# Eight transposes moved up SyncE's queue in a fused attention and mixer kernel

## The chip, the cores and the metric

The kernel runs on one core of one Trainium2 chip. The metric is the device time of one execution in microseconds. Five engines with a queue each take part: TensorE (PE, matmuls), VectorE (DVE), ScalarE (ACT), GpSimd (POOL, here mostly the issuer of loads that cast from float32 to bfloat16) and SyncE (SP, here the issuer of all DMA transposes and of the stores). All DMAs share the core's 16 DMA engines; the page lists SyncE's as queue q1 and GpSimd's as queue q0.

## The reference, cut to what matters

Eight batches of 3008 tokens. First a gated attention without softmax, then an MLP mixer over tokens and channels:

```python
scores = scale * np.matmul(z, z.transpose(0, 2, 1))    # z: (8, 3008, 64)
attn = np.maximum(scores, 0.0) ** 2
x = u * np.matmul(attn, v)                             # u, v: (8, 3008, 256)
h = np.maximum(x.transpose(0, 2, 1) @ w_tok1, 0.0) @ w_tok2    # d_tok = 256
y = x + h.transpose(0, 2, 1)
out = y + np.maximum(y @ w_ch1, 0.0) @ w_ch2           # d_ch = 1536
```

## The kernel before, in words

The 3008 tokens of a batch are cut into `NQ = 6` query blocks of 512 (the last has 448), and the keys into `NG = 6` groups of the same size. A block of scores (one query block, one key group) is made in two pieces of 1024 columns: TensorE multiplies (`sc`, L457), ScalarE takes the relu into a buffer `at` (L495), VectorE squares it in place (L503). Six `at` buffers go round. TensorE then multiplies the block by v into the accumulators of the query block (L684). Scores are symmetric, so from the second batch on a block above the diagonal is computed once and its mirror image is made by a DMA transpose on SyncE (`flip`, L550, issue at L554), from `at` into a buffer `fl`. The `at` buffer is free when its own product and its transpose are done. In batch 0 every block is computed directly.

When a query block is complete, VectorE adds its halves and multiplies by u (`gate`, L818 and L838), which gives `xT`. SyncE transposes this x (`turn_x`, L870, issue at L875, into `x_pair`), and VectorE makes sums of it (`x_sums`, L912, into `d_pair`); both feed the token mixer, which starts when the last block of the batch is done (`tok1`, L1017).

Inputs reach the core by GpSimd and are turned by SyncE: `load_z` (L129) and `turn_z` (L141, and L145 for the last tile), `load_u` (L248) and `turn_u` (L258); `load_v` (L220) and the weights (L267 to L289) are only loaded. `after` (L124) has GpSimd copy one column of a tensor into `mark`, so that everything behind it in GpSimd's queue waits until that tensor is there.

The order on each engine is written by a planner when the program is built: it keeps a model of the engines' times and emits instructions in the order that the model gives. Loads and turns do not come out of the model; they are hung on steps of the attention by hand. `at_group(n, f)` runs f when the planner begins group n, where n counts blocks of scores times v: `base` is the batch's first, `q * NG` the query block's. The engines themselves take the instructions of their queue strictly in that order and wait on semaphores, so the hand-set step decides only the place in the queue. `turn_u` for query blocks 2 to 5 of batch 0 and `turn_next_z` (the two halves of z of batch 1) are such steps. So is this list of loads, which is spread over steps from `begin` on and stands behind one mark:

```python
    items = [lambda c=c: load_v(1, c) for c in vorder]
    items += [lambda c=c: ask_w_tok1(c) for c in range(NG)]
    items += [lambda c=c: ask_w_tok2(c) for c in range(NG)]
    items += [lambda part=part: ask_w_ch(part) for part in range(4)]
    items += [lambda m=m: load_u(m // NQ, m % NQ) for m in (NQ, NQ + 1)]
    begin = 2 * NG + 3
    at_group(begin, lambda: after(zTs[1][:, KT, :1]))
```

The later u loads of batch 1 (`ask_u`) wait each for a mark and for a `ur` buffer, of which there are two, each free when its turn has landed. The program's functions are long; the ones that the text speaks of are those named here.

Of the kernel before, what the change touches and what calls it, by code (L numbers as in the profile page):

```python
# [57 lines left out]
def kernel(  # L58
# [22 lines left out]
    NQ = (S + QW - 1) // QW  # L81
    NG = KT // GK
# [39 lines left out]
    def after(column):  # L122

        nc.gpsimd.tensor_copy(mark[:column.shape[0], :1], column)  # L124

    def load_z(b, c):
        n = full_tiles[c]
        k = c * GK + 1
        nc.gpsimd.dma_start(out=zs[:, k:k + n, :], in_=rows_of(z[b], c))  # L129
        if n < GK:  # L130
            for r in range(2):
                nc.gpsimd.dma_start(
                    out=zs[r * TAIL:(r + 1) * TAIL, k + n, :], in_=last_rows(z[b]))
        loading(LOAD / 4)

    def turn_z(zT, half):


        n = KT // 2
        for k in (half * n, half * n + 1):  # L140
            nc.sync.dma_start_transpose(  # L141
                out=zT[:, k:k + n:2, :],
                in_=zs[:, k:k + n, :].rearrange("p t d -> p (t d)"))
        if half:
            nc.sync.dma_start_transpose(  # L145
                out=zT[:, KT, :], in_=zs[:, KT:, :].rearrange("p t d -> p (t d)"))
# [97 lines left out]
    def load_u(b, q):  # L244
        tag, n = u_home(b, q, "ur")
        ur = sb.tile([P, QW // P, D], BF16, tag=tag, name="ur", bufs=n)
        n = full_tiles[q]
        nc.gpsimd.dma_start(out=ur[:, :n, :], in_=rows_of(u[b], q))  # L248
        if n < QW // P:
            nc.gpsimd.memset(ur[TAIL:, n, :], 0.0)  # L250
            nc.gpsimd.dma_start(out=ur[:TAIL, n, :], in_=last_rows(u[b]))
        urs[b, q] = ur
        loading(LOAD)

    def turn_u(b, q):
        ur = urs.pop((b, q))
        uT = new_uT(b, q)
        nc.sync.dma_start_transpose(  # L258
            out=uT.rearrange("p t h s -> p (t h) s"),
            in_=ur.rearrange("p t d -> p (t d)"))  # L260
        on_sp(1.25)
        if b == 0 and q > 1:
            release("fl", [1], free["sp"] + 4.0)
# [1227 lines left out]
    def new_zT(b):  # L1491
        zTs[b] = sb.tile([P, KT + 1, P], BF16, tag="zT", name="zT", bufs=2)
# [12 lines left out]
    def on_sp(us):  # L1505
        start = max(free["sp"], pe[0])
        free["sp"] = start + shared(start, us)

    def turn_next_z(b, half):
        turn_z(zTs[b + 1], half)  # L1510
        on_sp(2.8 + 1.2 * half)

        for c in range(NG // 2 * half, NG // 2 * (half + 1)):
            turned[b + 1, c] = Done(pe[0] + 10.0)
        if half:
            turned[b + 1, NG // 2 - 1] = Done(pe[0] + 10.0)
# [4 lines left out]
    def at_group(n, f):  # L1521
        fetch.setdefault(n, []).append(f)
# [31 lines left out]
    def when_used(b, c, j):  # L1554
        ask(lambda: load_v(b + 1, c),
            lambda: used.get((b, vorder[j]), 0) == NQ)
# [3 lines left out]
    def ask_u(m, group):  # L1560
        at_group(group, lambda: ask(lambda: u_then_turn(m), lambda: len(uTs) > m - 2))

    def ask_z(b, group):
        at_group(group, lambda: new_zT(b))
        for j in range(NG):
            at_group(group, lambda j=j: ask(lambda: z_then_turn(b, j)))

    for b in range(B):
        base = b * NQ * NG
        for q in range(NQ):  # L1570
            m = b * NQ + q + 2
            if b == 0:
                if m < NQ:
                    at_group(base + NG, lambda m=m: load_u(m // NQ, m % NQ))
                late_turn = NQ * NG + 1 + 4 * (m - NQ) if m >= NQ else 2 * NG + (1, 2, 3, 4)[q]
                at_group(base + late_turn, lambda m=m: turn_u(m // NQ, m % NQ))
            elif m < 2 * NQ:
                ask_u(m, base + q * NG + 2)
        if b == 0:
            at_group(base + 2, lambda b=b: new_zT(b + 1))  # L1580
            for j in range(NG):
                at_group(base + 3 + j // 2, lambda b=b, j=j: load_z(b + 1, j))
                if j % 3 == 2:
                    at_group(base + 12 + 2 * (j // 3), lambda b=b, j=j: turn_next_z(b, j // 3))
        else:
            if b == 1:
                ask_z(2, base + HALF * NG - 1)
            if b + 1 < B:
                last, m = base + NQ * NG - 1, (b + 1) * NQ
                ask_u(m, last)  # L1590
                for j, c in enumerate(vorder):
                    at_group(last, lambda b=b, c=c, j=j: when_used(b, c, j))
                ask_u(m + 1, last)
                ask_u(m + 2, last)
                if b + 2 < B:
                    ask_z(b + 2, last)
                for k in range(3, NQ):
                    ask_u(m + k, last)
# [66 lines left out]
    items += [lambda c=c: ask_w_tok2(c) for c in range(NG)]  # L1665
    items += [lambda part=part: ask_w_ch(part) for part in range(4)]
    items += [lambda m=m: load_u(m // NQ, m % NQ) for m in (NQ, NQ + 1)]
    begin = 2 * NG + 3
    at_group(begin, lambda: after(zTs[1][:, KT, :1]))
    for k, item in enumerate(items):  # L1670
        at_group(begin + k * (NQ * NG - NG - begin + 1 + W_LATER) // len(items), item)
# [171 lines left out]
```

## Time and profile before

| what | value |
|---|---|
| three runs, us | 1133.4, 1129.81, 1132.12 |
| median, us | 1132.12 |
| profiled execution, its own time, us | 1130.13 |
| its span, first to last instruction, us | 1128.3 |
| granted TensorE clock | 1.000 |
| busy share PE, DVE, ACT, POOL | 99%, 69%, 58%, 14% |
| HBM read, written | 65.40 MB, 24.64 MB |
| DMA traffic, mean over the span | 147 GB/s |

The page gives for each engine its busy time; for a group of instructions the source line, the engine, the tiles (out<-in), the count, the busy time and what ended the idle time before it. A row of the timeline has its start, its length, and in brackets the idle time of the engine just before it with its releaser. Rows marked SPq are DMA issues of SyncE's queue: their length is how long the issue kept SyncE. A landing is when the DMA's data has arrived.

### The profile page before, as it was taken

The numbers are of one execution on the slowest core, as the hardware profiler recorded it, in microseconds if no ns is written. First come the engines' busy times: TensorE is split into PE (matmuls) and PEld (weight loads), VectorE is DVE, ScalarE is ACT, GpSimd is POOL, SyncE is SP. The second block draws the span as 40 slices with busy tenths as digits, with TensorE's granted clock in tenths as the row PEclk, the third lists the DMA queues.
The fourth block names the chain that finished last, engine by engine and source line by source line (L and its number), as shares of the span: only waits on it lengthen the run. The fifth ranks groups of instructions, "written<-read, shape, count | busy, mean of one in ns | idle before, by whom it ended". The sixth has DMA issues, their size and how long they took to land.

```text
span 1128.3 us, 26908 instructions
## 1 busy us (share of the span) xinstructions
PE 1112.0 (99%) x10965; PEld 676.1 (60%) x10965; DVE 782.6 (69%) x1849; ACT 654.1 (58%) x817; POOL 162.9 (14%) x388
## 2 busy tenths in 40 slices
PE   8999999999999999999999999999999999999998
PEld 3444465666557665576555765557655576556676
DVE  6888756875767757578566785667756777557774
ACT  7997535535855358545665456753666526753353
POOL 4140010221002110022100320003110120000000
PEclk9999999999999999999999999999999999999999
DMA  9699965688977879879697896957969779594223
GB/s 171 97 200 193 199 129 118 112 156 165 180 143 131 163 149 183 139 145 186 141 149 143 143 198 133 190 112 136 201 145 161 127 145 175 135 164 97 61 65 87
DMA packets 464620, 165.52 MB, mean 147 GB/s; under 512 B 433072, under 2 KB 446960, under 8 KB 464496
## 3 DMA queue, kind: packets, MB, share of 16 engines
q1 hardware_dynamic: 436640, 131.11, 58.2%
q0 software_dynamic: 27344, 32.32, 20.5%
q8 instruction: 85, 1.39, 0.5%
q10 hardware_dynamic: 512, 0.38, 0.1%
q14 instruction: 39, 0.32, 0.1%
HBM read 65.40 MB, written 24.64 MB: 80 GB/s over the span
## 4 chain that ended last, share of the span: by engine, by line
PE 89%; DVE 5%; DMA 4%; ACT 1%; issue 1%; SPq 0%; ACTq 0%; DVEq 0%
PE acc L684 37%; PE hp L1117 21%; PE xb L1245 9%; PE zb L1245 7%; PE sc L457 6%; PE a_ps L1017 3%; DMA fl<-at 3%; PE op L1331 3%; PE h_ps L1061 2%; DVE xT L1070 2%; ACT at L495 1%; PE first_acc L601 1%; DMA zT<-zr 1%; DVE at L503 1%; DVE res L1366 0%
## 5 line engine op out<-in xcount | busy, mean ns | idle before, releaser
L1155 ACT ACTIVATE h2pre<-hp 128x1024 bf16<-128x1024 f32 (+1 forms) x277 | 267.6, 1011 | 262.8 <-PE hp L1117 224.9
L684 PEld LDWEIGHTS <-v_sb 64*128 64x128 bf16 x4418 | 239.7, 94 | 217.6 <-issue 1.5
L684 PE MATMUL acc<-at,v_sb 64*128 64x512 bf16 (+1 forms) x2738 | 339.2, 374 | 0.0
L495 ACT ACTIVATE at<-sc 128x1024 bf16<-128x1024 f32 (+1 forms) x290 | 287.2, 1027 | 80.9 <-PE sc L457 58.4
L503 DVE TENSOR_TENSOR at<-at 128x1024 bf16<-128x1024 bf16 (+1 forms) x290 | 198.3, 688 | 113.2 <-ACT at L495 109.0
L1117 PE MATMUL hp<-xT,w_ch_sb 128*128 128x512 bf16 (+1 forms) x1152 | 270.6, 375 | 0.3
L684 PE MATMUL acc<-fl,v_sb 64*128 64x512 bf16 (+1 forms) x1680 | 192.0, 367 | 0.3 <-ACT at L495 0.3
L1117 PEld LDWEIGHTS <-w_ch_sb 128*128 128x128 bf16 x1152 | 105.9, 98 | 99.8 <-issue 2.7
L457 PE MATMUL sc<-zT 64*128 64x512 bf16 (+1 forms) x732 | 131.5, 359 | 7.8 <-ACT at L495 5.4
L1245 PEld LDWEIGHTS <-hsum 128*128 128x128 bf16 x1944 | 115.9, 98 | 20.1 <-issue 0.2
L1245 PEld LDWEIGHTS <-h2pre 128*128 128x128 bf16 x1458 | 88.8, 98 | 18.9
L812 ACT COPY cp<-acc 128x512 f32<-128x512 f32 (+1 forms) x94 | 54.9, 584 | 72.1 <-PE acc L684 59.7
L818 DVE TENSOR_TENSOR cp<-acc,cp 128x512 f32<-128x512 f32 (+1 forms) x94 | 63.5, 675 | 37.3 <-ACT cp L812 36.8
L1196 DVE TENSOR_TENSOR hsum<-h2pre 128x512 bf16<-128x512 bf16 (+1 forms) x132 | 53.0, 405 | 42.2 <-ACT h2pre L1155 36.7
L483 ACT ACTIVATE at<-sc 128x512 bf16<-128x512 f32 (+3 forms) x152 | 55.9, 443 | 44.9 <-PE sc L457 38.9
L457 PEld LDWEIGHTS <-zT 64*128 64x128 bf16 x732 | 42.5, 94 | 52.0 <-issue 12.2
L1245 PE MATMUL xb<-w_mix_sb,hsum 128*128 128x128 bf16 x972 | 68.6, 219 | 0.0
L534 DVE TENSOR_TENSOR at<-at 128x512 bf16<-128x512 bf16 (+3 forms) x152 | 41.6, 322 | 35.9 <-ACT at L483 35.8
L1282 DVE TENSOR_TENSOR ro<-xb,u_sb 128x256 f32<-128x256 f32 (+1 forms) x132 | 52.7, 399 | 17.2 <-PE xb L1245 16.2
L838 DVE TENSOR_TENSOR xT<-cp,uT 128x512 bf16<-128x512 f32 (+1 forms) x94 | 62.4, 664 | 0.6
L124 POOL CAST mark<-at 128x1 f32<-128x1 bf16 x24 | 8.0, 332 | 335.5 <-DVE at L503 335.5
L1070 DVE TENSOR_TENSOR xT<-xT,h_ps 128x1024 bf16<-128x1024 bf16 (+1 forms) x48 | 54.9, 1170 | 0.1
(88 smaller groups left out, 982.7 us busy)
## 6 DMA issues: line engine op xcount, KB each, us to landing
out_dram<-ro SPq DMA_DIRECT2D x37, 512.0 KB, 2.9
v_sb<-in_v_dram POOLq DMA_DIRECT2D x40, 256.0 KB, 5.0
ur<-in_u_dram POOLq DMA_DIRECT2D x40, 256.0 KB, 4.9
w_tok_sb<-in_moe_w_tok_dram POOLq DMA_DIRECT2D x10, 256.0 KB, 10.7
zs<-in_z_dram POOLq DMA_DIRECT2D x35, 64.0 KB, 3.8
at<-at SPq DMA_TRANSPOSE x114, 3.1
out_dram<-ro SPq DMA_DIRECT2D x7, 256.0 KB, 2.4
fl<-at SPq DMA_TRANSPOSE x105, 4.6
```

What stands on the lines that cost most here:

```text
L457: nc.tensor.matmul(sc[:, r, c0:c1], zT[h, k:k + P], zT[h, m + c0:m + c1], start=True, stop=True)
L483: nc.scalar.activation(a3[:, i, c0:c1], sc[:, r, c0:c1], ACT.Relu, scale=inv_S)
L495: nc.scalar.activation(view, sv, ACT.Relu, scale=inv_S)
L503: nc.vector.tensor_mul(view, view, view)
L684: nc.tensor.matmul(o, vs[blk.b, g][rows, i, dh * P:(dh + 1) * P], rhs, start=(dh, h) not in blk.begun, stop=stop, skip_group_check=True)
L812: nc.scalar.copy(cp[:, :W], acc[:, 1, :W])
L818: nc.vector.tensor_add(cp[:, :W], acc[:, 0, :W], cp[:, :W])
L838: nc.vector.tensor_mul(xT[:, dh, :full * P].rearrange("p (t s) -> p t s", s=P), acc[:, :full * P].rearrange("p (t s) -> p t s", s=P), uT[: ...
L1070: nc.vector.tensor_add(to, to, h[:, :, :n * P].rearrange("p h (s t) -> p h t s", t=n))
L1117: nc.tensor.matmul(hp[:, r, :W], w_ch1_sb[:, dc, cc * P:(cc + 1) * P], xT[:, dc, :W], start=(dc == 0), stop=(dc == DT - 1))
L1155: nc.scalar.activation(h2[:, :, :W], hp[:, :, :W], ACT.Relu)
L1245: nc.tensor.matmul(to[:, i * P:(i + 1) * P], lhs, weights[:, c2, :], start=(first_use and c2 == 0 and i == 0), stop=(c2 == CHT // 2 - 1), ...
```

## The change

Three hand-set steps move. The turns of u of query blocks 2 to 5 of batch 0 go from steps 13 to 16 to steps 11, 12, 12 and 13; the two halves of z of batch 1 from steps 12 and 14 to steps 10 and 11; the list of loads begins at step 12 and not 15.

```diff
@@ -1572,7 +1572,7 @@
             if b == 0:
                 if m < NQ:
                     at_group(base + NG, lambda m=m: load_u(m // NQ, m % NQ))
-                late_turn = NQ * NG + 1 + 4 * (m - NQ) if m >= NQ else 2 * NG + (1, 2, 3, 4)[q]
+                late_turn = NQ * NG + 1 + 4 * (m - NQ) if m >= NQ else NG + (5, 6, 6, 7)[q]
                 at_group(base + late_turn, lambda m=m: turn_u(m // NQ, m % NQ))
@@ -1581,7 +1581,7 @@
             for j in range(NG):
                 at_group(base + 3 + j // 2, lambda b=b, j=j: load_z(b + 1, j))
                 if j % 3 == 2:
-                    at_group(base + 12 + 2 * (j // 3), lambda b=b, j=j: turn_next_z(b, j // 3))
+                    at_group(base + NG + 4 + j // 3, lambda b=b, j=j: turn_next_z(b, j // 3))
@@ -1665,7 +1665,7 @@
     items += [lambda part=part: ask_w_ch(part) for part in range(4)]
     items += [lambda m=m: load_u(m // NQ, m % NQ) for m in (NQ, NQ + 1)]
-    begin = 2 * NG + 3
+    begin = 2 * NG
     at_group(begin, lambda: after(zTs[1][:, KT, :1]))
```

In SyncE's queue, as the two programs are built, the order after the first half of z and the first of the four u turns becomes: second half of z (three transposes), three u turns, x of the second block, x of the third. Before it was: x of the second block, one u turn, second half of z, two u turns, x of the third. Further on in the queue one transposed score block and one u turn of the next batch trade places. GpSimd's queue keeps its order. On VectorE some sums of x and of a weight move by a few places; on TensorE two neighbouring groups of eight matmuls trade places, and the rest of the program has the same order on every engine.

## The prediction

> **What bounds the kernel now.** I read the page first. TensorE (PE) is busy for nearly the whole span, so only time in which PE stands still can be won.
>
> ```profile
> PE 1112.0 (99%) x10965; PEld 676.1 (60%) x10965; DVE 782.6 (69%) x1849; ACT 654.1 (58%) x817; POOL 162.9 (14%) x388
> ```
>
> Next I asked what PE waits for between 100 and 120 us, where batch 0 ends and the second batch begins, and beside it ScalarE's (ACT's) instructions there.
>
> ```profile
> PE sc L457 <- ACT at L495: 4.6, 3, 2.3
> ...
> 108.13 1.94 ACT L495 ACTIVATE at<-sc 128x1024 bf16<-128x1024 f32 x2 [2.99 <-DMA fl<-at]
> 110.89 1.94 ACT L495 ACTIVATE at<-sc 128x1024 bf16<-128x1024 f32 x2 [0.82 <-DVE at L503]
> 115.16 1.94 ACT L495 ACTIVATE at<-sc 128x1024 bf16<-128x1024 f32 x2 [2.34 <-DMA fl<-at]
> ```
>
> PE's three waits (2.32, 0.42 and 1.87 us, at 109.20, 111.96 and 116.24) sum to 4.61 us. They are the largest block of PE idle time that is left: 3.3 us more lie before 14 us, where nothing is edited, 0.47 at 139.8 behind VectorE, and the rest of the span has no single gap over 0.8. ACT is late because a score buffer `at` is only free once SyncE's turn of it (`flip`, L554) has landed. The third step is the chain of waits, which shows these turns, and the timeline of SyncE, which shows where they queue.
>
> ```profile
> 98.84 9.19 DMA fl<-at
> 108.08 0.04 issue
> 108.13 0.67 ACT at L495
> 108.80 6.26 DMA fl<-at
> ...
> 26.43 1.23 SPq L875 DMA_TRANSPOSE x_pair<-xT  x1
> 27.85 2.54 SPq L141 DMA_TRANSPOSE zT<-zs  x2
> 30.49 1.26 SPq L258 DMA_TRANSPOSE uT<-ur  x1
> 42.22 1.23 SPq L875 DMA_TRANSPOSE x_pair<-xT  x1
> 43.55 1.26 SPq L258 DMA_TRANSPOSE uT<-ur  x1
> 44.97 2.54 SPq L141 DMA_TRANSPOSE zT<-zs  x2
> 47.60 1.19 SPq L145 DMA_TRANSPOSE zT<-zs  x1
> ...
> 87.59 6.64 SPq L554 DMA_TRANSPOSE fl<-at  x1
> ```
>
> Call the second batch's first five turned blocks F1 to F5. From the landings in the trace: issued at 87.59, 97.39, 98.84, 105.92, 108.80; landed at 97.11, 101.13, 108.03, 110.78, 115.06. Their squares on VectorE were done at 87.56, 91.31, 93.40, 95.68, 97.83, so F2 to F5 stood 5 to 11 us in SyncE's queue. The head of that queue is F1, which kept SyncE for 6.64 us where F2 kept it 1.36. What F1 met is in GpSimd's timeline and in the DMA queues from 60 to 66 us:
>
> ```profile
> 50.09 0.47 POOL L124 CAST mark<-zT 128x1 f32<-128x1 bf16 x1 [26.78 <-DMA zT<-zs]
> 79.03 0.55 POOL L248 DMA_DIRECT2D ur<-in_u_dram  x1 [1.18 <-DMA w_tok_sb<-in_moe_w_tok_dram]
> 98.58 0.53 POOL L248 DMA_DIRECT2D ur<-in_u_dram  x1 [7.96 <-DMA uT<-ur]
> ...
> q0 software_dynamic: 591, 1.08, 95.0%
> q1 hardware_dynamic: 592, 0.15, 18.2%
> ```
>
> GpSimd stands for 26.78 us, then starts 24 loads of v, weights and u; the last lands at 95.37. While they run, the turns (q1) get 18% of the DMA engines.
>
> **The change part by part.** (1) Six turns on SyncE move ahead of the x at 42.22: first the three of z (44.97, 46.28, 47.60), then the three of u (43.55, 48.88, 50.31). Their data is there: z landed by 23.84, u by 28.79. SyncE is free at 31.75. At 1.25 us each and 0.1 between, z's last turn issues at 34.5 and lands 2.4 later (as at 47.60: landed 49.96), so at 36.9. The u turns issue until 38.4, before the x is ready at 42.2: nothing waits on SyncE. GpSimd's mark is the next on its queue; it ends its wait at 37.0 and not 50.1: 13.1 us sooner.
>
> (2) All 24 loads move with it, since GpSimd's order is the same. Nothing else holds them: the v buffers were read by 10 us, the weights have room of their own. The last lands at 95.4 - 13.1 = 82.3, before F1.
>
> (3) What the loads now lie beside: 37 to 82 us in place of 50 to 95. PE is busy 10.00 of each 10 us from 20 to 100, with the loads as without them, so their shadow costs PE nothing where it was; the squares take 691 ns on average at 30 to 48, with GpSimd idle, and 689 at 52 to 80 beside it. Cost nothing, as long as the x turns still land ahead of their readers (third rival).
>
> (4) Small moves: two groups of eight matmuls swap on PE, so that F2 is first wanted at 100.9 and not 101.76; the sums of one x go 2.5 us back on VectorE; four weight sums (L956, 0.35 us each) go ahead to about 85 us, where VectorE is busy 5.35 of 7 us (80 to 87): its gaps hide them, and without the gaps they would hold F1 by 1.4 us, which F5's 3 us in hand below take up. The step from which the loads are planned (`begin`) does not bind GpSimd. Zero in all.
>
> (5) The gain. How late each F was: its landing less the PE stall by then. F3 had to land by 108.03 - 2.32 = 105.7, F4 by 110.78 - 2.74 = 108.0, F5 by 115.06 - 4.61 = 110.45. Now, with the engines free at 87.6: F1 issues at 87.6 and lands at 91.3 (F2's 3.7 us). The u turn of the next batch behind it lands at 92.4, which frees a buffer, and GpSimd's u load follows at 92.5 where it stood at 98.58; with its 6.2 us it lands at 98.7. F2 goes out at 92.1 (ready 91.3, behind an x) and shares that load's time: landing between 96 and 99, wanted by PE at 100.9. F3 is caught as it was (in the trace it landed 3.3 us behind this load): 102.0, 3.7 before it is due. F4, at the 2.2 us between two full-rate turns: 104.2, due 108.0. A u turn (1.1): 105.3. F5: 107.5, due 110.45. So the three stalls go. The bounds of this sum: 4.61 us if F5 meets nothing, 2.7 if it repeats its whole last stall of 1.87. I take 4.4, close to the free end, because F5 has 3 us in hand. What is late next: the 0.47 at 139.8, which moves along.
>
> The profiled execution took 1130.13 us around a span of 1128.3; it becomes 1130.13 - 4.4 = 1125.7. The median of the three runs shown is 1132.12, 2.0 above it: 1132.12 - 4.4 = **1127.7**.
>
> **The rivals.** *The second u load still catches F5.* The u turn ahead of F5 now lands at about 105.3, and the next u load (109.33 before) follows at once: 5.5 us, to 110.8. In the trace F5 landed 0.26 us behind that load. For: F5's issue, 102.5 to 104, lies close before it, and 6.3 us (its time before) from 104 is 110.3. Against: F5's data is through at 107.5, when the load's first packets start. Left are 0.4 to 1.9 us of stall, and if F3 is caught twice up to 3.5: 1127.9 to 1131.0, likeliest 1129.4. [...]
>
> *No change.* The wait ends sooner, but the engines are as full at 87 us, because the loads spread out or F1 to F5 are held by VectorE, which has no gap between 87.5 and 106. For: its squares keep F5 back until 97.8. Against: that is 11 us before F5 was issued. 1132.1, within the scatter of the runs.
>
> *Slower: x behind the loads.* The x of the second block, issued at 42.22, landed after 2.7 us in clean engines; now it goes 5 us into the loads, as the x at 54.95 did before, which took 16.3. At that it lands at 58.5; its first reader on VectorE stood at 63.77 (d_pair, L912), and behind that reader stand the squares. It decides at 21.5 us of landing time. If turns got nothing until the loads are over (82), VectorE would stand for 18 us and PE for some 14, after the two score buffers in hand (one lasts it 2.15 us): 1146. Against: 18% is what they got, and the two next x, at 54.95 and 67.68, have readers at about 79 and 91.5.
>
> **How the numbers follow.** A measurement of this kernel can tell about 0.3%, 3.4 us, from no change (the three runs lie 3.6 apart). Forecast (0.57): 3.6 to 4.6 won, 1127.5 to 1128.5. F5 caught (0.26): 1127.9 to 1131.0. No change (0.08). Slower (0.09). Faster by over 0.3%: nine tenths of the first case and a fifth of the second, rounded up to 0.57; slower by over 0.3%: the last case, 0.09; within: 0.34. The range goes from everything won with the quickest run's scatter, 1132.12 - 4.61 - 2.31 = 1125.2, up to the end of the second case and a little scatter, 1131.4.
>
> **What would show it.** Right: the mark on GpSimd near 37 us, the last of the 24 loads down by 83, F1 keeping SyncE under 2 us, no wait of `sc` on ACT over 0.5 us between 100 and 117. The second rival to the forecast would show as the mark early and those waits still there; F5 caught, as one wait near 110 with a u load landing beside it; the slower one, as VectorE idle before L912 near 64 us. Wrong in kind would be any new wait of PE before 100 us, or a difference that arises after 150 us, where the order on every engine is as before.

## The result and the profile after

| | before | after |
|---|---|---|
| median of 22 runs each, us | 1132.32 | 1126.08 |
| lowest and highest, us | 1127.47, 1138.0 | 1122.93, 1131.93 |
| ratio, 95% interval | | 0.9938, 0.9923 to 0.9952 |
| profiled execution, its own time and span, us | 1130.13, 1128.3 | 1127.49, 1125.7 |

The change makes the kernel faster by 6.2 us between the medians; 4.4 were forecast, and the interval spans 5.4 to 8.7. The two profiled executions are only 2.6 us apart, because that of before lies 2.2 below its median and that of after 1.4 above. Where runs of the kernel before are averaged further down, one of 1147.44 us, 1.7% above the quickest of its 28, is left out.

The page's first lines of the kernel after: PE's busy time is as before, the span is shorter.

```profile
span 1125.7 us, 26909 instructions
...
PE 1112.3 (99%) x10965; PEld 676.5 (60%) x10965; DVE 782.3 (69%) x1849; ACT 654.0 (58%) x817; POOL 162.9 (14%) x388
```

SyncE's timeline of the kernel after, from 30 to 44 and from 86 to 110 us (start, how long the issue kept SyncE, operation, tiles, count). Each row with x2 or x3 is that many issues in a run.

```profile
31.56 2.54 SPq L141 DMA_TRANSPOSE zT<-zs  x2
34.19 1.18 SPq L145 DMA_TRANSPOSE zT<-zs  x1
35.47 5.09 SPq L258 DMA_TRANSPOSE uT<-ur  x3
41.87 2.02 SPq L875 DMA_TRANSPOSE x_pair<-xT  x1
...
87.24 1.62 SPq L554 DMA_TRANSPOSE fl<-at  x1
...
92.92 9.83 SPq L554 DMA_TRANSPOSE fl<-at  x3
102.84 2.72 SPq L258 DMA_TRANSPOSE uT<-ur  x1
105.65 1.58 SPq L554 DMA_TRANSPOSE fl<-at  x1
```

F1 keeps SyncE 1.62 us (6.64 before). F2, F3 and F4 are the three issues from 92.92 on, then comes the u turn at 102.84, then F5 at 105.65. GpSimd's timeline shows the mark, the last of the 24 loads and the second u load:

```profile
38.60 0.27 POOL L124 CAST mark<-zT 128x1 f32<-128x1 bf16 x1 [15.33 <-DMA zT<-zs]
...
68.53 0.54 POOL L248 DMA_DIRECT2D ur<-in_u_dram  x1 [1.09 <-DMA w_tok_sb<-in_moe_w_tok_dram]
...
108.08 0.53 POOL L248 DMA_DIRECT2D ur<-in_u_dram  x1 [5.29 <-DMA uT<-ur]
```

The wait for the mark ends at 38.6, not 50.1, and the load issued at 68.53 lands at 82.39. Of PE's waits from 95 to 130 us one is left, where 4.61 us stood:

```profile
PE sc L457 <- ACT at L495: 0.9, 1, 0.9
```

All idle gaps of PE over 40 ns sum to 11.66 us before (3.33 up to 20 us, 5.08 from 100 to 150, 3.24 after 300) and 8.70 after (2.86, 1.62, 4.22). So in this pair the gain lies where the change works, 3.46 us of it, and 1.0 is lost again to small waits of later batches, which other executions of both kernels show too.

### The profile page after: what moved, and what is told of

Its sections match the earlier page's. It is cut to its first block, busy times and chain, and to the rows that moved or that the text cites. A ratio compares the mean times of both kernels' runs of the same rounds, so it can differ in the third digit from the quotient of the medians.

```text
span 1125.7 us, 26909 instructions
## 1 busy us (share of the span) xinstructions
PE 1112.3 (99%) x10965; PEld 676.5 (60%) x10965; DVE 782.3 (69%) x1849; ACT 654.0 (58%) x817; POOL 162.9 (14%) x388
## 3 DMA queue, kind: packets, MB, share of 16 engines
q1 hardware_dynamic: 436640, 131.11, 58.5%
## 4 chain that ended last, share of the span: by engine, by line
PE 87%; DVE 6%; DMA 4%; ACT 1%; issue 1%; SPq 1%; ACTq 0%; DVEq 0%
PE acc L684 37%; PE hp L1117 21%; PE xb L1245 9%; PE zb L1245 6%; PE sc L457 6%; PE a_ps L1017 3%; PE op L1331 3%; DMA fl<-at 3%; PE h_ps L1061 2%; DVE xT L1070 2%; ACT at L495 1%; PE first_acc L601 1%; DMA zT<-zr 1%; DVE ro L1282 1%; DVE res L1366 0%
## 5 line engine op out<-in xcount | busy, mean ns | idle before, releaser
L457 PE MATMUL sc<-zT 64*128 64x512 bf16 (+1 forms) x732 | 131.6, 359 | 4.1 <-ACT at L495 2.1
L457 PEld LDWEIGHTS <-zT 64*128 64x128 bf16 x732 | 42.4, 94 | 47.7 <-issue 8.0
```

The lines of the kernel that those rows point to most:

```text
L457: nc.tensor.matmul(sc[:, r, c0:c1], zT[h, k:k + P], zT[h, m + c0:m + c1], start=True, stop=True)
```

## The experiments

Each was timed in five rounds beside runs of the kernel before, except the two first, which are one profiled execution each. A ratio is always to the kernel before. "Second u load" is the load of `ur` that GpSimd issues once the u turn between F3 and F5 has landed.

### A second look at both kernels

The kernel before, unchanged:

> The kernel before once more, for a second profile. The stretch theory (all that the change wins are PE's waits for score buffers from 100 to 130 us, and their size differs from run to run because the u loads meet other turns): this profile shows between 4 and 10 us of them, its own time differs from the first profile's by about that difference, and the rest of PE's idle time is within 1.5 us of the 7.0 us there. The elsewhere theory (the change also wins in later batches): PE's idle time after 150 us is 2 us or more above the 4.2 us that the profile after the change shows there.

It took 1136.26 us. PE's rows with a wait over 1 us near the second batch's start, and four windows around them (from:to, width, busy time and count on PE, PEld, DVE, ACT, POOL, then the granted clock, the DMA share and GB/s):

```profile
109.20 0.39 PE L457 MATMUL sc<-zT 64*128 64x512 bf16 x2 [2.19 <-ACT at L495]
120.15 0.41 PE L457 MATMUL sc<-zT 64*128 64x512 bf16 x2 [4.77 <-ACT at L495]
```

```profile
106.74:110.16 3.42, 1.23 (x14) 0.54 (x11) 0.95 (x3) 1.94 (x2) 0.53 (x1) 1.00 0.87 193
110.16:113.57 3.41, 3.41 (x20) 1.56 (x17) 2.97 (x8) 1.94 (x2) 0.00 (x0) 0.50 1.33 97
...
116.98:120.40 3.42, 0.25 (x4) 0.14 (x5) 0.27 (x1) 1.32 (x2) 0.00 (x0) 1.00 1.27 202
120.40:123.81 3.41, 3.41 (x26) 2.10 (x23) 3.15 (x6) 2.50 (x4) 0.00 (x0) 0.50 1.23 220
```

Two things differ from the first profile of this kernel. The waits sum to 6.96 us, not 4.61: the second u load took 9.1 us (109.29 to 118.37) where it had taken 5.5, and F5 (issued at 108.94) landed 0.6 us behind it. And behind each wait the granted clock falls to one half for 3.41 us, from 110.16 and from 120.40 on; in the first profile it stood at 1.00 up to the end of the program. So the expectation that the two executions differ by about the difference of their waits (2.35 us) failed: they lie 6.1 us apart, and the clock's falls are a part of that: less its waits, the stretch that "The size" reads took 32.5 us in this look and 29.5 in the first.

The kernel after, unchanged:

> The kernel after once more, for a second profile. The stretch theory: PE's waits on ScalarE from 100 to 130 us come to less than 1.5 us again (0.9 in the first), and the quicker runs of this kernel differ from this one by small waits behind 130 us. The elsewhere theory: the waits after 150 us differ from the first profile's by more than those before it.

1127.92 us, clock 1.00, no wait of PE over 0.5 us between 100 and 130. The second u load is issued at 108.16, 3.76 us behind F5. PE's idle time behind 150 us is 1.1 us above the first profile's (5.3 and 4.2), while in the stretch from 100 to 150 it is 1.2 below (0.5 and 1.6): executions of this kernel scatter by about 1 us in either place.

### The loads earlier, the turns where they were

```diff
-    begin = 2 * NG + 3
-    at_group(begin, lambda: after(zTs[1][:, KT, :1]))
+    begin = 2 * NG - 1
+    at_group(begin, lambda: after(recent[0]))
```

The mark is on a square of batch 0 that is ready at 30; no turn moves by hand.

> The kernel before, but the mark in front of the list of loads reads a score buffer that is squared at step 11 and not the last turn of z; the turns keep their old places behind the second block's x. The loads start near 38 us. Theory that the earlier loads bring the gain: ratio to before 0.992 to 0.996, F1 keeps SyncE under 2.5 us and lands by 93, PE waits less than 1.5 us from 100 to 117. Theory that the turns' own place in SyncE's queue brings it: 0.998 to 1.002. Against both: the turns of z and u now run beside the loads and take some 16 us; z is not read before 84, u of the fifth block not before 76, so no new wait. If one comes, ratio over 1.

1134.07 us, ratio 1.0009 (0.9989 to 1.0029): nothing won. The loads start at 30.84 (near 38 was expected) and the waits between 100 and 117 are gone, but a new one is there, as large. PE's and VectorE's rows with their waits, and SyncE's row that explains them:

```profile
80.91 0.56 PE L457 MATMUL sc<-zT 64*128 64x448 bf16 x2 [4.61 <-DVE cp L818]
```

```profile
79.36 0.29 DVE L912 TENSOR_TENSOR d_pair<-x_pair 128x256 bf16<-128x256 bf16 x1 [5.14 <-DMA x_pair<-xT]
```

```profile
45.14 17.16 SPq L141 DMA_TRANSPOSE zT<-zs  x2
...
72.28 11.01 SPq L875 DMA_TRANSPOSE x_pair<-xT  x3
```

Two turns of z keep SyncE for 17 us beside the loads, so the x of the third block, which goes out at 54.95 in the kernel before, stands behind them until 72.28, and VectorE's sums wait for it. This is the prediction's slower rival, in a kernel where it decides: not one x that crawls, but the turns ahead of it. Moving the turns out of the loads' way is what makes earlier loads worth anything.

### The loads later again, the turns early

The changed kernel with 36 small copies on GpSimd between its mark and the loads. They took 16.5 us where about 11 were meant, so the loads start at 57.89 and not 39.

```diff
+    def stand(n):
+        nc.gpsimd.memset(mark[:, 1:], 0.0)
+        for i in range(n):
+            a, b = (1, 16) if i % 2 else (16, 1)
+            nc.gpsimd.tensor_copy(mark[:, b:b + 15], mark[:, a:a + 15])
+    at_group(begin, lambda: stand(36))
```

> The kernel after, but GpSimd does 36 idle copies of 15 columns between the mark and the first load, some 11 us, so that the loads start near 50 us as they did before; turns, plan and every other queue stay as after. Theory of the earlier loads: the gain is gone, ratio 0.998 to 1.002, F1 keeps SyncE for 5 us or more, PE waits 4 us or more from 100 to 130. Theory of the turns' place: the gain stays, 0.992 to 0.996.

1139.4 us, ratio 1.005 (1.0031 to 1.0069). F1 keeps SyncE 10.15 us, and PE waits longer than before the change:

```profile
108.39 0.61 PE L457 MATMUL sc<-zT 64*128 64x512 bf16 x2 [5.21 <-ACT at L495]
111.40 1.89 PE L684 MATMUL acc<-fl,v_sb 64*128 64x512 bf16 x8 [2.40 <-DMA fl<-at]
```

The clock is at one half for 10.24 us from 106.86 on. With the loads 7 us later than in the kernel before, the early turns don't help; what F1 meets decides.

The same with 20 matmuls of zeros (their sum adds nothing) put ahead of the score that waits, so that PE has work in part of its wait:

```diff
+            if unit == ((1, 1, LAST), 1):
+                keep_busy(20)
```

> The kernel stand_11us (loads 19 us later than after the change, PE stands 5.2 us at 108 and 2.4 us at 111, mean granted clock 0.995) with 20 matmuls of zero weights into an open accumulator (they add zero) ahead of the score product that waits 5.2 us: PE works through most of that wait. Theory that a long wait of PE costs more than its length, because the granted clock then falls to 0.5 for some 3.4 to 10 us: the waits of sc shrink by about 4.3 us with no loss, the clock's drop near 107 to 117 goes, the mean clock rises to 0.997 or more and the time falls 3 to 5 us below stand_11us (ratio to before 1.000 to 1.003). Theory that a wait costs its length alone: ratio 1.004 to 1.007 as without the matmuls, whatever the clock's record says.

1136.41 us, ratio 1.0013 (0.999 to 1.0035): some 4 us quicker, each against its own session's runs of the kernel before (the two intervals overlap by 0.0004). The waits are 1.15 and 2.69 us, since the zeros fill part of them, and the clock fell for 6.83 us and not 10.24. That the zeros won these 4 us isn't shown. From PE's 160th score matmul (L457) to its 200th, a stretch that holds both waits, the profiled execution with zeros took 40.04 us and the one without 39.84; of the 5.1 us between the two executions, 3.6 had arisen before that stretch. What a fall of the clock costs is read better from that same stretch in all runs; see "The size" below.

The same copies, 11 of them (5.0 us), without the zeros: loads from 43.37, the last down at 84.12.

> The kernel after with 11 idle copies on GpSimd between mark and loads (0.46 us each in stand_11us), so the loads start near 44.5 us and the last lands near 87.5, just when F1 is issued at 87.2. Theory that F1 to F5 must meet no loads: nearly all of the gain stays, ratio 0.992 to 0.997, PE's waits from 100 to 130 under 2.5 us, F1 keeps SyncE under 4 us. Theory that the gain falls with the start of the loads, so much for each us: half between after (0.994) and stand_11us (1.005), 0.996 to 0.999.

1125.57 us (6 runs), ratio 0.9917 (0.9889 to 0.9945), no wait of PE over 0.5 us near 100 to 130. The x of the second block lands 2.7 us after its issue, where it takes 16.3 in the kernel after, yet nobody had waited for it. So 4 us of the 13 were to spare. The interval overlaps that of the kernel after, and which of the two is quicker isn't settled.

### Half of the turns each

Only z's turns and `begin` edited; the u turns stay at steps 13 to 16:

> The kernel before with two of the three edits: the turns of z at steps 10 and 11, the loads from step 12; the u turns keep steps 13 to 16. As built, the planner now sets the second block's x behind all turns all the same. The mark ends near 37 us. Theory of the earlier loads with the turns out of their way: ratio 0.992 to 0.996, PE's waits on ScalarE from 100 to 130 under 1.5 us, no wait near 81. Theory that the u turns' steps are needed: 0.998 or more.

1130.5 us, ratio 0.9972 (0.995 to 0.9994). The mark ends at 36.6 and the loads run from 36.82 to 89.63. One wait of PE is left, 5.28 us at 117.78. F3 is no longer late; F5, issued at 107.22, lands at 116.6 behind the second u load (107.55 to 115.91):

```profile
117.78 0.61 PE L457 MATMUL sc<-zT 64*128 64x512 bf16 x2 [5.28 <-ACT at L495]
```

Only the u turns edited, z and `begin` as before:

> The kernel before with the u turns' edit alone. As built, x of the second block goes behind all turns here too, with the last z turn near 39 us and so the loads from 41 us. The theory: ratio 0.992 to 0.997, the stretch as after the change. Theory that the z turns' own steps are needed: 0.998 or more.

1127.99 us, ratio 0.9955 (0.9932 to 0.9979). Loads from 41.86 to 82.62; one wait of 2.07 us at 112.59, again at F5 (issued 105.00, second u load 105.82):

```profile
112.59 0.39 PE L457 MATMUL sc<-zT 64*128 64x512 bf16 x2 [2.07 <-ACT at L495]
```

Both halves are the prediction's first rival, as it was described, and both missed the expected stretch without waits.

### Another mark

The changed kernel again, and two variants that should have been its equals, in one session:

> The changed kernel again, beside the two variants below. Ratio to the kernel before 0.992 to 0.996; no wait of PE over 1 us between 100 and 117; the x of the second block issued at about 42 and landing near 58, with the loads from about 39 to 82.

1126.88 us, ratio 0.9941 (0.9913 to 0.9968), one wait of 1.0 us at 127.9.

The mark on the x of the second block, so that this x lands clean (the list of loads is held to the same step):

```diff
-    at_group(begin, lambda: after(zTs[1][:, KT, :1]))
+    at_group(2 * NG + 4, lambda: after(xs[0, 1][:, 0, 0, :1]))
```

> The changed kernel with its mark on the x of the second block instead of z: the loads start behind that x's landing, near 44.7. If loads only have to be over when F1 goes out, the last lands at 82.3 + 5.6 = 87.9 or earlier (less of SyncE's work lies beside them), F1 keeps SyncE under 3 us, F5 lands by 110.4 and PE has no wait over 0.5 us between 100 and 117: the same time as the changed kernel within 0.2%, and the x lands in under 4 us. The rival, that each us which the loads lose is paid at F1: F1 keeps SyncE 4 us or more, one wait of PE of 1 us or more comes back, and the ratio to the kernel before is 0.996 or above.

1131.68 us, ratio 0.9979 (0.9953 to 1.0006). The x landed after 2.7 us, but the loads (47.9 to 95.2, where 87.9 at the latest was expected) still met F1, which went out at 91.36 and kept SyncE 3.80 us. Waits of 0.43, 0.35, 0.41 and 4.12 us came back, the last at F5.

The mark on the last of the four u turns (`uTs[0, NQ - 1]`, step `2 * NG + 2`):

> The changed kernel with its mark on the last of the four u turns instead of z: the loads start near 41.5, the x of the second block still lies in them. By either theory the last load lands near 84, F1 is free, and the time is that of the changed kernel within 0.2%. If the turns beside the first loads cost something that the trace hides, this one gains as much as the one that waits for x; if not, all three agree.

1131.35 us, ratio 0.9984 (0.9964 to 1.0005). Both theories failed here: the loads were early enough (42.40 to 82.97), F1 was free (2.50 us), and yet most of the gain was gone. PE's row for F5 (one more wait, of 0.30 us, is at F2) and SyncE's:

```profile
116.49 0.61 PE L457 MATMUL sc<-zT 64*128 64x512 bf16 x2 [5.50 <-ACT at L495]
```

```profile
93.28 7.73 SPq L554 DMA_TRANSPOSE fl<-at  x2
101.10 1.26 SPq L258 DMA_TRANSPOSE uT<-ur  x1
102.45 4.53 SPq L554 DMA_TRANSPOSE fl<-at  x2
```

Beside the rows of the kernel after this shows what had been overlooked: here the u turn stands behind two blocks (F2, F3), in the kernel after behind three. It is the trade of places of a turned block and a u turn that the change brings along; z_only, u_only and loads_behind_x lack it as well, stand_5us has it. With F4 behind the u turn, the second u load starts 1.2 to 2.3 us sooner than in the three looks at the kernel after (105.89 against 108.08, 108.16 and 107.06), and F5 has lost its lead over it.

### That trade alone

The kernel before, with the u turn moved from step 41 to step 42:

```diff
-                late_turn = NQ * NG + 1 + 4 * (m - NQ) if m >= NQ else 2 * NG + (1, 2, 3, 4)[q]
+                late_turn = NQ * NG + (1, 6)[m - NQ] if m >= NQ else 2 * NG + (1, 2, 3, 4)[q]
```

> The kernel before with one trade of places alone: the u turn of the next batch that stands between the third and the fourth turned block (F3, F4) in SyncE's queue goes one place back, behind F4, as the change has it too. The mark, the loads and the turns ahead of them stay late. Theory: this trade is a part of the gain of its own, since the second u load starts behind that turn's landing and takes F5's engines. Then F1 still keeps SyncE about 6.6 us and the wait of 2.2 to 2.4 us near 109 stays (F3), the second u load starts 1.5 to 3 us later, near 111, F5 lands by 113 and its wait (1.87 us in the first profile, 4.77 in the second) falls under 0.5: 1.5 to 4 us won, ratio 0.9965 to 0.9985. The rival, that only the earlier loads count: F4 and F5 are late with F3 anyway, the second u load overlaps F5 as before, waits of 4.6 to 7 us in all stay, ratio 0.999 to 1.001.

1130.87 us, ratio 0.9974 (0.9949 to 0.9999), 2.4 us between the medians; the interval only just leaves out no gain. PE's one wait, and SyncE's rows:

```profile
110.00 0.39 PE L457 MATMUL sc<-zT 64*128 64x512 bf16 x2 [3.08 <-ACT at L495]
```

```profile
87.33 6.73 SPq L554 DMA_TRANSPOSE fl<-at  x1
...
97.92 10.24 SPq L554 DMA_TRANSPOSE fl<-at  x3
108.25 1.26 SPq L258 DMA_TRANSPOSE uT<-ur  x1
109.61 1.36 SPq L554 DMA_TRANSPOSE fl<-at  x1
```

F1 still meets the late loads and the wait for F3 stays (3.08 us, more than the 2.2 to 2.4 expected), but F5's is gone: it lands 3.8 us after its issue, and the second u load is issued at 111.86, 2.25 us behind it.

### What the runs say together

F5 against the second u load, in every profile. The fourth column says when F5 landed, counted from the first packet of that load (a minus: ahead of it); the packets start 1.6 to 2.9 us behind the load's issue.

| kernel | loads over before F1 | F5 issued ahead of the u load, us | F5's landing against the load's first packet, us | F5, issue to landing, us | PE's wait for it, us |
|---|---|---|---|---|---|
| before, first and second look | no | 0.53, 0.35 | 2.8, 8.1 | 6.3, 10.0 | 1.87, 4.77 |
| z_only | yes, by 0.1 | 0.33 | 7.5 | 9.4 | 5.28 |
| u_only | yes | 0.82 | 3.2 | 6.4 | 2.07 |
| loads_behind_u | yes | 0.43 | 7.5 | 9.9 | 5.50 |
| loads_behind_x | no | 0.50 | 5.6 | 8.4 | 4.12 |
| u_turn_behind_f4 | no | 2.25 | -1.2 | 3.8 | none |
| after (three looks) | yes | 2.43, 3.76, 3.70 | -0.7, -1.1, -0.9 | 3.9 to 5.0 | none |
| stand_5us | yes | 3.54 | -0.9 | 4.7 | none |
| loads_early_turns_late | yes | 3.64 | -0.9 | 4.8 | none |
| stand_11us, with and without zeros | no | 2.26, 2.15 | -1.0, -0.3 | 3.8, 3.8 | 0.17, none |

In the first five rows the u turn stands ahead of F4, in the other five behind it. Every profile without the trade has F5 caught, every one with it has F5 down before the load's first packet; no lead lies between 0.82 and 2.15 us. In u_only what is late in the caught F5 isn't its data. The last packet of 256 bytes in SyncE's queue starts at 108.43, 0.2 us behind the load's first, and from then until 110.16 the queue moves nothing but packets of 4 bytes (q0 is GpSimd's queue, q1 SyncE's; packets, MB, share of the engines' time; from 108.5 to 110.1 us):

```profile
q0 software_dynamic: 26, 0.05, 53.8%
q1 hardware_dynamic: 10, 0.00, 0.9%
```

Yet F5's landing is recorded only at 111.41, 2.98 us behind the start of that last packet. So in this profile the landing isn't the moment when the data had arrived.

The wait for F3 in turn goes with the loads' end in these profiles: 2.32, 2.19 and 3.08 us in the two looks at the kernel before and in u_turn_behind_f4, where the loads aren't over before F1, and none in z_only, u_only and the kernel after, where they are. The change has both parts: the three kernels with earlier loads and without the trade (z_only, u_only, loads_behind_u) have ratios of 0.9955 to 0.9984 (mean 0.9970), the trade alone 0.9974, both together 0.9938 and 0.9941. That the parts add up (3.0 and 2.6 thousandths, against 5.9 to 6.2) fits within these intervals; it isn't proved by them. The profiled executions of z_only and loads_behind_u are the slowest of their twelve and that of loads_behind_x the slowest but one, 3.3 to 5.8 us above their medians, so these kernels mostly pay less for F5 than the 4.1 to 5.5 us in the table; u_only's is the third quickest of its twelve.

## Why the prediction was right, and where its working was not

**The mark, the loads, the x.** The wait for the mark ended 1.6 us later than the 37.0 forecast, since z's last turn took 4.3 us from issue to landing and not 2.4. The last load landed at 82.39 (82.3 forecast); it had only to be down before F1. The x of the second block landed at 58.14 (58.5 forecast from the x at 54.95), and its reader didn't wait: the slower rival's condition did not arise, for the reason given. (The 18% that the prediction gives the turns is a share of the engines' time; of the bytes in that window they had 0.15 of 1.23 MB, 12%.)

**F1 to F4.** F1 landed at 92.64, F2 at 96.81, F3 at 103.02, F4 at 106.64, against 91.3, 96 to 99, 102.0 and 104.2, all ahead of their due times. The stalls of 2.32 and 0.42 went as argued.

**F5: the mechanism held, the lead wasn't earned.** F5 was to come through because its data would be done when the load's first packets start, both at 107.5, with the u turn ahead of it down at 105.3. So it went, 2 us later: F5 landed at 109.58, 0.9 before it was due, and the load, issued at 108.08, had its first packet at 110.24. But the sum's own times left F5 no lead at all. F3 landed 1.0 late and F3 to F4 took 3.6 us (2.2 forecast), so the u turn behind them landed at 107.52, 2.2 late, and held the load back; F5 itself went out at 105.65 and not between 102.5 and 104. That the errors left 0.7 to 1.1 us in F5's favour in all three looks is in part luck. And what holds the load back is the trade of places. The sum used the new order, F4 ahead of the u turn, without pricing it: the text on the change names the trade, the prediction's list of small moves, put at zero in all, doesn't. Alone it won 2.4 us (0.1 to 5.8 by the interval).

**The size.** Two terms of the sum were too small. The waits were priced from one execution, 4.61 us; the second look at the same kernel had 6.96, so the mean of the two is 5.8, of which after keeps 0.6 (0.86, 0 and 1.04 in three looks). And the clock's falls were not in the sum: the first profile had none. Their price can be read from a stretch that holds the same 306 matmuls in every kernel but the one with zeros, from PE's 160th score matmul (L457) to its 200th. Less the waits within, it took 28.9 us in the five profiles without a wait there, 29.5 in the first look at the kernel before (three waits, no fall), 30.8 to 31.2 in the four with one fall of 3.41 us, and 32.5 in the second look, with two. So a fall of 3.41 us added some 1.4 to 2.3 us to the waits here, by which of the two first figures it is counted from.

How often the clock falls differs between executions. Over 27 runs of the kernel before, in the session of after_beside, the mean granted clock was 0.9972, over the 11 of the kernel after 0.9987; estimated from these means, the time at half speed cost 3.2 and 1.5 us (0.0028 and 0.0013 of some 1130). The difference, 1.7, is an upper estimate: the runs with a clock of 1.000 average 1131.4 before (5 runs) and 1125.4 after (4 runs), which is still 6.0 apart, and leaves the clock only 0.3 of the 6.3 between that session's medians. The waits' 5.2 and the clock's 0.3 to 1.7 give 5.5 to 6.9 us, with 6.2 and 6.3 measured. How much of it is the clock stays open. That nothing else is needed fits the stretch from the 160th up to the 216th score matmul, near 130 us: 42.5 and 47.9 us before, 38.4, 37.3 and 38.5 after, 7.1 between the means.

**The rivals.** The second u load catching F5 is real: it is what happens in four of the experiments, and in these runs no kernel without the trade escapes it. The price put on it (0.4 to 1.9 us, up to 3.5) was too low; it measures 2.1 to 5.5 in the profiled executions. In five of the six caught cases F5's landing is recorded 0.2 to 0.7 us behind the load's landing (118.97 behind 118.37, 115.31 behind 115.14), in one, u_only, 0.8 ahead of it, 3.2 behind its first packet. "No change" is refuted by the interval.

## What to carry to other kernels

When an edit of an order by hand runs through a planner, list every pair that trades places further on and price each: here a side effect at 103 us was worth about as much as the 13 us that the loads gained (2.6 against 3.0 thousandths). Give a transfer that PE waits for a lead over the next large load on the same DMA engines, not only clear engines before it: here F5 came through with 2.15 us or more and was caught with 0.82 or less, also in the three kernels whose loads were over before F1. So look at which of the two is issued first and by how much. And take the price of a wait that hangs on a shared resource from more than one execution (4.61 and 6.96 us here).

## What the runs showed of the hardware

In these traces the granted clock fell by steps of time. The second look at the kernel before has two falls to one half, from 110.16 and from 120.40 on, 10.24 us apart, and each lasts 3.41 us; in stand_11us one lasts 10.24 us, three times as long, and in the run with zeros one lasts 6.83, twice as long. In the first profiles of the two kernels the clock falls only at the program's end, 1122.99 us (before) and 1119.57 us (after) behind its first record, which is 329 and 328 steps of 3.413 us. In the second look PE stood idle for 2.19 and 3.17 us of the steps that ended where the two falls began (106.74 to 110.16 and 116.98 to 120.40). In the first profiles it was idle for 1.72 us of a step at most (before, 114.52 to 117.93), and no fall followed. The length of a wait alone did not decide it here: in the second look the wait of 2.19 us lay within one step and a fall followed. In the first look a wait of 2.32 us lay across the edge at 107.69, with 0.81 us of idle time ahead of it and 1.51 behind it, and none followed:

```profile
104.28:107.69 3.41, 2.60 (x26) 1.07 (x21) 2.06 (x6) 0.86 (x1) 0.00 (x0) 1.00 1.17 161
107.69:111.10 3.41, 1.90 (x18) 1.11 (x19) 1.89 (x5) 2.15 (x3) 0.53 (x1) 1.00 1.18 265
```

Where the edges lie differs from run to run (the first record is at 5.29 us in the first profile before and at 5.06 in that after). In u_only a wait of 2.07 us, over at 112.59, had a fall behind it: the mean clock was 1.00 from 112 to 113.5 and 0.51 from 113.5 to 117.

The same u load of 256 KB took from 5.5 us (first look at the kernel before) to 9.2 us (loads_behind_u) from issue to landing. A turned block beside it (F5 in the first five rows of the table) took 6.3 to 10.0 us, and 3.8 to 5.0 us ahead of it (the other five rows).
